# Three more zero matmuls in TensorE's lead-in, and four between the first transform's second group and the first product

## The chip, the cores and the metric

The kernel runs on one core of a Trainium2 chip. The metric is the device time of one execution in microseconds (us), as a median over several executions; lower is better.

## The reference, cut to what matters

```
def A(x, w_r, w_i):                     # x: 2048 x 512
    X = rfft2(x.astype(float32))        # over both axes: 2048 x 257
    return irfft2(X * (w_r + 1j * w_i)).astype(bfloat16)

def B(x, w1, b1, w2, b2):               # w1: 2048 x 1792, w2: 1792 x 2048
    h = layernorm(x)                    # over the 512 columns
    u = gelu(einsum("bsd,sf->bdf", h, w1) + b1)
    return (einsum("bdf,fs->bds", u, w2) + b2).transpose(0, 2, 1)

g = sigmoid((x * gate_w).sum(-1, keepdims=True))
out = g * A(x) + (1 - g) * B(x)
```

Inputs, weights and output are bfloat16; A and B get the same x.

## The kernel before, in words

**The layout.** The 2048 rows are cut into sixteen blocks of 128, j = 4q + r, where r is the row's number modulo 4. Everything that belongs to one r (four blocks, 512 KB of x) is loaded and handled together, in the order r = 0, 1, 2, 3.

**The layer-norm branch.** VectorE (DVE) takes mean and variance of each block (L461, L462), ScalarE (ACT) takes the root (L471), DVE the reciprocal and shift (L475, L476). The normalized block h is then written by ACT (L485), or by DVE (L479) for blocks 0, 8 and 4. The *products* of the first matrix multiplication (L655) are 14 column tiles ft times 16 blocks j = 224 matmuls of 128x512. The first six tiles go pairwise through the blocks as these come: twelve products for blocks 0 and 8, six for block 4, six for 12, six for 1 and so on. Each finished tile goes through gelu on ACT (L669). The second multiplication (L929) is again 224 such matmuls.

**The Fourier branch.** For each r, DVE makes four sums and differences of the blocks (L493, L494, L499, L500), and TensorE (PE) multiplies them by tables in four groups dq of four matmuls (L512 to L515, function `fa`): the *first transform* of r. Each group fills one of two PSUM buffers with the tag "fa", which ACT empties (L518). DVE then works on the results (L525 to L532, radix4 at L551 to L564). The second transform (L620 to L623, evicted at L627), the reversal of the filter's rows (L705), the inverse transforms (L841 to L844, L837 and L911 to L915) follow, with DVE's multiplication and butterflies between them.

**The lead-in.** Before any data are there, `warm` (L350 to L353) issues thirteen 128x512 matmuls on a tile that DVE has set to zero (L314). Nothing reads their result. A second zeroed tile, `s9` (L315, L319), gets its real contents only late in the kernel, by a DMA (L803).

**What sets the order.** All work is written down as tasks with an engine, a book duration, what they read and write, a priority (lower goes first), and the PSUM buffers that they take and give back (`add`, L149). `order` (L170) plays these through in book time before the program is built: whenever an engine is free, the ready task of the lowest priority number starts. What an engine executes on the chip is this order, fixed; only waits on the chip decide when. A task that follows one of another engine is ready 0.15 book-us after it, and on DVE 0.10 after one of its own. Book durations that the text uses: 0.42 for each zero matmul (L355), 0.2158 for a product (`mm(512)`), 0.33 for a group of the first transform, 0.49 for its eviction. Priorities on PE: lead-in -5, first transform 0, second transform 2, inverse transforms 3 and 4, reversal 5, products 10 and up, so products fill the time that all else leaves free.

Of the kernel before, what the change touches and what calls it, by code (L numbers as in the profile page):

```python
# [14 lines left out]
F32 = mybir.dt.float32  # L15

P = 128
S = 2048
D = 512
# [117 lines left out]
class Plan:  # L137
# [11 lines left out]
    def add(self, eng, dur, emit, reads=(), writes=(), prio=0.0, alloc=(), free=(), nbytes=0, after=()):  # L149
        t = Task()  # L150
        t.eng, t.dur, t.emit, t.prio = eng, dur, emit, prio
        t.alloc, t.free, t.nbytes = tuple(alloc), tuple(free), nbytes
        t.users, t.end, t.ready = [], None, 0.0
        deps = set(after)
        for k in reads:
            if k in self.last_w:
                deps.add(self.last_w[k])
            self.readers.setdefault(k, []).append(t)
        for k in writes:
            if k in self.last_w:  # L160
                deps.add(self.last_w[k])
            deps.update(self.readers.get(k, ()))
            self.last_w[k] = t
            self.readers[k] = []
        deps.discard(t)
        t.deps = deps
        self.tasks.append(t)
        return t
# [79 lines left out]
def act(n, ptr=0):  # L248
    return 0.065 + 0.09 * ptr + n / 1200.0
# [12 lines left out]
def kernel(  # L262
# [14 lines left out]
    V, A, T = nc.vector, nc.scalar, nc.tensor  # L277
# [15 lines left out]
    def ps(shape, dt, tag, bufs):  # L293
        return psum.tile(shape, dt, tag=tag, name=tag, bufs=bufs)
# [4 lines left out]
    add = pl.add  # L299
    t = {}  # L300
# [49 lines left out]
    def warm():  # L350
        pw = ps([P, D], F32, "fa", 2)
        for _ in range(NWARM):
            T.matmul(pw[:], lhsT=t["warm"][:, 0:P], rhs=t["warm"], start=True, stop=True)  # L353
    NWARM = 13
    add("PE", 0.42 * NWARM, warm, reads=["warm", "xs"], writes=["warmed"], prio=-5, alloc=["fa"], free=["fa"])  # L355

    def presq():
# [23 lines left out]
    for b in range(2):  # L381
        add(("SP", "ACT")[b], 0.5, ld_w1(0, slice(b, 4, 2), (None, A)[b]), writes=[("w1", 0, 4 * b), ("w1", 0, 4 * b + 8)], prio=(0.5, -4)[b],
            alloc=() if b else ["wa"], nbytes=393216, after=[a0])
# [62 lines left out]
    for r in range(4):  # L446
# [3 lines left out]
        for b, qs in enumerate(groups):  # L450
# [32 lines left out]
            for j in js:  # L483
                if j in HACT:
                    add("ACT", act(512, 2), lambda j=j: A.activation(t["h"][:, j // 4, j % 4, :], t["x"][:, j // 4, j % 4, :], ActF.Identity,  # L485
                                                                  bias=t["nmr"][:, j:j + 1], scale=t["rstd"][:, j:j + 1]),
                        reads=xb + [("rstd", *g)] + mvk, writes=[("h", j)], prio=-0.5 + 0.1 * r)
# [19 lines left out]
        for dq in range(4):  # L507
            def fa(r=r, dq=dq):
# [8 lines left out]
                free=["xf"] if dq == 3 else ())  # L517
            add("ACT", act(512), lambda r=r, dq=dq: A.copy(t["X"][:, :, r, :, dq, :], t["pa", r, dq][:]),  # L518
                reads=[("pa", r, dq)], writes=[("X", r, dq)], prio=0, free=["fa"])
# [77 lines left out]
    for lt in (1, 0):  # L597
# [5 lines left out]
        writes=[("Z", 0, 0), ("Z", 0, 1)], prio=3.1)  # L603
# [8 lines left out]
    for lt in (0, 1):  # L612
        for e in (0, 2, 1, 3):
            for c in range(2):
# [13 lines left out]
                           t["pb", lt, e, c][:].rearrange("p s b i -> p s i b"))  # L628
                add("ACT", act(512), fbev, reads=[("pb", lt, e, c)], writes=[("B", lt, e)], prio=1.8, free=[tag])


    def biasT():
        pb = t["pbias"] = ps([P, 32], F32, "fa", 2)
        T.matmul(pb[:, 0:NFT], lhsT=t["b1b"][:], rhs=t["flip"][:, P - NFT:P], start=True, stop=True)
        for r in range(4):
            T.matmul(pb[:, 16 + 4 * r:20 + 4 * r], lhsT=t["b2b"][:, r::4], rhs=t["flip"][:, P - 4:P], start=True, stop=True)
# [26 lines left out]
    for n, (ft, j) in enumerate(order):  # L663
# [3 lines left out]
                       prio=10 + n * 1e-3, alloc=[bank] if j == jorder[0] else (), free={NF - 1: ["wa"], NF + 3: ["wb"], NFT - 1: ["wb"]}.get(ft, ()) if last else ()))  # L667
        if last:
            gelus.append(add("ACT", act(512, 1), lambda ft=ft: A.activation(  # L669
                t["gl"][:, ft, :], t["u", ft][:], ActF.Gelu_apprx_tanh, bias=t["b1f"][:, ft:ft + 1], scale=1.0),  # L670
                reads=[("u", ft), "b1f"], writes=[("gl", ft)] + ([("xf", (ft - 6) // 4)] if ft >= 6 else []), prio=0.5,
                free=[bank]))
# [3 lines left out]
    for r in range(4):  # L676
# [3 lines left out]
            reads=["gw"], writes=xk, prio=6)  # L680
# [5 lines left out]
        reads=[("xg", q, r) for q in range(4) for r in range(4)], writes=["g"], prio=5, after=gelus[0:1])  # L686
# [25 lines left out]
    def wfn():  # L712
# [6 lines left out]
        reads=["pwn"], writes=wtk, prio=3, free=["fa"])  # L719
# [90 lines left out]
    for lt in range(2):  # L810
# [5 lines left out]
        if lt == 0:  # L816
            add("SP", 0.5, lambda: dma(t["B"][0:1, 0].rearrange("p e (c v) l -> p (e c) (v l)", c=2), t["s8"][:]),
                reads=["s8"], writes=[("T", 0, 0), ("T", 0, 1)], prio=0, nbytes=8192)
# [83 lines left out]
    for grp in groups:  # L902
        for j in grp:
# [19 lines left out]
            for n, cs in enumerate(parts):  # L923
                for ft in range(NFT):
                    def m2(ft=ft, j=j, q=q, r=r, n=n, cs=cs):
# [6 lines left out]
                        alloc=[("acc", "fa")[n]] if ft == 0 else (), after=m1t[-16:-15] if ft == 0 else ())  # L932
# [24 lines left out]
            else:  # L957
# [6 lines left out]
                for n, cs in enumerate(parts):  # L964
                    def fin(j=j, n=n, cs=cs):
# [3 lines left out]
                        free=[("acc", "fa")[n]])  # L969
# [42 lines left out]
```

## Time and profile before

| | |
|---|---|
| time, median of 3 runs | 135.7 us (135.46 to 136.01) |
| span of the profiled execution, first to last instruction | 134.9 us |
| PE busy | 128.1 us, 95% of the span |
| DVE busy | 115.2 us, 85% |
| ACT busy | 82.3 us, 61% |
| mean granted TensorE clock | 0.987 |
| HBM read and written | 20.93 MB and 2.10 MB |

The profile gives the span of the profiled execution and no total time of its own; the median of the timed runs lies 0.8 us above that span. In the profile, a row of the timeline has start, duration, engine, line, operation, output and inputs, shape and count, and in brackets how long the engine had stood idle before and what ended that. Matmuls are pipelined, so durations of neighbours overlap; the pace of PE is the distance between their starts. The table of stretches lists, for each stretch of time, the busy time of each engine, then the granted TensorE clock (PEclk), the share of DMA and its GB/s. The chain of waits follows the work that ended last back to what released it.

### The profile page before, as it was taken

The numbers are of one execution on the slowest core, as the hardware profiler recorded it, in microseconds if no ns is written. First come the engines' busy times: TensorE is split into PE (matmuls) and PEld (weight loads), VectorE is DVE, ScalarE is ACT, GpSimd is POOL, SyncE is SP. The second block draws the span as 40 slices with busy tenths as digits, with TensorE's granted clock in tenths as the row PEclk, the third lists the DMA queues.
The fourth block names the chain that finished last, engine by engine and source line by source line (L and its number), as shares of the span: only waits on it lengthen the run. The fifth ranks groups of instructions, "written<-read, shape, count | busy, mean of one in ns | idle before, by whom it ended". The sixth has DMA issues, their size and how long they took to land.

```text
span 134.9 us, 2171 instructions
## 1 busy us (share of the span) xinstructions
PE 128.1 (95%) x763; PEld 72.2 (53%) x777; DVE 115.2 (85%) x294; ACT 82.3 (61%) x159; POOL 0.2 (0%) x4
## 2 busy tenths in 40 slices
PE   6949999999999999999999999999999999999991
PEld 2234465645544576644445445557766755655590
DVE  2987999999999994499999999998696899999531
ACT  4036679998999999994222007237993776574200
POOL 0000000000000000000000000000000000000000
PEclk9995999999999999999999999999999999999999
DMA  4999999996399928999701940000000003303021
GB/s 128 246 367 363 362 355 346 345 233 84 100 351 322 150 39 317 373 418 404 293 6 35 415 174 0 5 2 2 0 0 0 5 0 155 152 9 158 16 101 39
DMA packets 17110, 23.18 MB, mean 172 GB/s; under 512 B 1078, under 2 KB 14540, under 8 KB 17100
## 3 DMA queue, kind: packets, MB, share of 16 engines
q1 hardware_dynamic: 16540, 22.39, 51.2%
q10 hardware_dynamic: 560, 0.66, 1.5%
q8 instruction: 6, 0.10, 0.3%
q14 instruction: 4, 0.03, 0.1%
HBM read 20.93 MB, written 2.10 MB: 171 GB/s over the span
## 4 chain that ended last, share of the span: by engine, by line
PE 61%; DMA 27%; SPq 9%; issue 1%; DVE 0%
PE acc L929 35%; PE acc L655 14%; DMA wa<-in_B_w_dram 12%; DMA wt<-in_A_w_i_dram 9%; SPq L303 9%; DMA wt<-in_A_w_r_dram 5%; PE fa L837 1%; PE fb L837 1%; PE fa L929 1%; PE fa L623 1%; PE fb L623 1%; PE fb L911 1%; PE fa L911 1%; PE fa L705 0%; PE fa L841 0%
## 5 line engine op out<-in xcount | busy, mean ns | idle before, releaser
L929 PE MATMUL acc<-gl,wb 128*128 128x512 bf16 (+1 forms) x123 | 31.0, 373 | 0.3
L655 PE MATMUL acc<-h,wb 128*128 128x512 bf16 x124 | 29.0, 379 | 0.1
L929 PE MATMUL acc<-gl,wa 128*128 128x512 bf16 (+1 forms) x94 | 23.4, 372 | 0.1
L929 PEld LDWEIGHTS <-wb 128*128 128x128 bf16 x136 | 14.8, 114 | 9.9 <-DMA wb<-in_B_w_dram 0.3
L655 PEld LDWEIGHTS <-wb 128*128 128x128 bf16 x128 | 12.4, 98 | 13.1
L655 PE MATMUL acc<-h,wa 128*128 128x512 bf16 x62 | 17.7, 394 | 1.0 <-DMA wa<-in_B_w_dram 0.9
L949 ACT ACTIVATE x<-acc,ombb,omg 128x512 bf16<-128x512 f32 x14 | 10.7, 776 | 11.2 <-PE acc L929 11.2
L929 PEld LDWEIGHTS <-wa 128*128 128x128 bf16 x102 | 11.5, 114 | 8.8
L655 PEld LDWEIGHTS <-wa 128*128 128x128 bf16 x96 | 9.8, 102 | 11.2 <-issue 1.3
L669 ACT ACTIVATE gl<-acc,b1f 128x512 bf16<-128x512 f32 x12 | 8.6, 715 | 8.9 <-PE acc L655 8.8
L461 DVE BATCH_NORM_STATS2 stats<-x 128x6 f32<-128x512 bf16 x16 | 10.8, 672 | 3.0 <-DMA x<-in_A_x_dram 3.0
L518 ACT CAST X<-fa 128x512 bf16<-128x512 f32 x16 | 8.9, 585 | 5.5 <-PE fa L515 5.3
L485 ACT ACTIVATE h<-x,nmr,rstd 128x512 bf16<-128x512 bf16 x13 | 9.6, 804 | 1.2 <-DVE nmr L476 1.2
L683 ACT ACTIVATE x<-x 128x512 bf16<-128x512 bf16 x16 | 10.2, 673 | 0.0
L655 PE MATMUL fb<-h,wa 128*128 128x512 bf16 x31 | 9.4, 395 | 0.0
L920 ACT ACTIVATE eo<-fa,g 128x512 bf16<-128x512 f32 x8 | 5.5, 686 | 4.8 <-DVE x L955 3.8
L353 PE MATMUL fa<-xp 128*128 128x512 bf16 x13 | 5.5, 612 | 1.2 <-DVE xp L314 1.2
L955 DVE TENSOR_TENSOR x<-x,eo 128x512 bf16<-128x512 bf16 x14 | 5.4, 418 | 0.5 <-ACT x L949 0.5
L920 ACT ACTIVATE eo<-fb,g 128x512 bf16<-128x512 f32 x8 | 5.5, 683 | 0.0
L808 ACT CAST s<-fa 8x512 bf16<-8x512 f32 x1 | 0.6, 574 | 7.9 <-PE fa L806 7.9
L627 ACT CAST B<-fb 128x512 bf16<-128x512 f32 x8 | 5.3, 661 | 0.0
L627 ACT CAST B<-fa 128x512 bf16<-128x512 f32 x8 | 5.2, 650 | 0.0
(167 smaller groups left out, 236.3 us busy)
## 6 DMA issues: line engine op xcount, KB each, us to landing
wb<-in_B_w_dram SPq DMA_DIRECT2D x8, 512.0 KB
wb<-in_B_w_dram SPq DMA_DIRECT2D x4, 1024.0 KB
wa<-in_B_w_dram SPq DMA_DIRECT2D x3, 1024.0 KB
wa<-in_B_w_dram SPq DMA_DIRECT2D x3, 768.0 KB
x<-in_A_x_dram SPq DMA_DIRECT2D x3, 512.0 KB
out_dram<-x SPq DMA_DIRECT2D x3, 512.0 KB
rot<-dft_ti SPq DMA_DIRECT2D x1, 736.5 KB
rot<-dft_ta SPq DMA_DIRECT2D x4, 160.0 KB
```

Source lines behind the costliest of these rows:

```text
L303: (eng or nc.sync).dma_start(out=out_ap, in_=in_ap)
L353: T.matmul(pw[:], lhsT=t["warm"][:, 0:P], rhs=t["warm"], start=True, stop=True)
L461: V.bn_stats(out=t["stats"][:, j, :], in_=t["x"][:, j // 4, j % 4, :])
L485: add("ACT", act(512, 2), lambda j=j: A.activation(t["h"][:, j // 4, j % 4, :], t["x"][:, j // 4, j % 4, :], ActF.Identity, bias=t["nmr"][ ...
L518: add("ACT", act(512), lambda r=r, dq=dq: A.copy(t["X"][:, :, r, :, dq, :], t["pa", r, dq][:]), reads=[("pa", r, dq)], writes=[("X", r, dq ...
L627: A.copy(t["B"][:, lt, e, 2 * c:2 * c + 2, :].rearrange("p s (i b) -> p s i b", b=4), t["pb", lt, e, c][:].rearrange("p s b i -> p s i b"))
L655: T.matmul(t["u", ft][:], lhsT=w[:, j // 4, j % 4, c * P:(c + 1) * P], rhs=t["h"][:, j // 4, j % 4, :], start=(j == jorder[0]), stop=(j == ...
L669: gelus.append(add("ACT", act(512, 1), lambda ft=ft: A.activation(t["gl"][:, ft, :], t["u", ft][:], ActF.Gelu_apprx_tanh, bias=t["b1f"][:, ...
L683: A.activation(t["x"][:, q, r, :], t["x"][:, q, r, :], ActF.Copy, accum_out=t["glog"][:, 4 * q + r:4 * q + r + 1])
L920: A.activation(t["eo", j][:], t["i3", j][:], ActF.Copy, scale=t["g"][:, j:j + 1])
L929: T.matmul(t["y", j, n][:, cs], lhsT=w[:, o, 512 * q + r:512 * q + 512:4], rhs=t["gl"][:, ft, cs], start=(ft == 0), stop=(ft == NFT - 1))
L949: A.activation(tbuf(j).rearrange("p h d -> p (h d)"), t["y", j, 0][:], ActF.Identity, bias=t["ombb2"][:, j:j + 1], scale=t["omg"][:, j:j + 1])
```

## The change

The lead-in gets sixteen zero matmuls in place of thirteen, and its book cost, 0.42 times that number, grows with it. A new PE task `fill` of four matmuls on the zeroed `s9` becomes ready when group dq = 1 of the first transform of r = 0 is done. Its book cost is 0.1, its priority 4, and it takes a PSUM buffer of the tag "fb" and gives it back. No result of it is read.

```
-    NWARM = 13
+    NWARM = 16
     add("PE", 0.42 * NWARM, warm, reads=["warm", "xs"], writes=["warmed"], prio=-5, alloc=["fa"], free=["fa"])
...
+    def fill():
+        pw = ps([P, D], F32, "fb", 2)
+        for _ in range(4):
+            T.matmul(pw[:], lhsT=t["s9"][:, 0:P], rhs=t["s9"][:], start=True, stop=True)
+    add("PE", 0.1, fill, reads=["warm", ("pa", 0, 1)], writes=["warmed"], prio=4, alloc=["fb"], free=["fb"])
```

## Prediction, made before the result was known

> **What bounds the kernel now.** I read the page first (busy shares and slices), then the list of waits, then the timelines of PE and DVE side by side at the places where PE takes DVE's results, and last the chain of waits.
>
> ```profile
> PE   6949999999999999999999999999999999999991
> ...
> DVE  2987999999999994499999999998696899999531
> ...
> PEclk9995999999999999999999999999999999999999
> ```
>
> PE is full from the fourth slice on, and DVE is as full until about 50 us: two engines in lockstep. The granted clock has one dip. In finer stretches (last columns: PEclk, DMA share, GB/s):
>
> ```profile
> 6.00:9.50 3.50, 1.60 (x12) 0.71 (x11) 3.40 (x11) 1.07 (x2) 0.00 (x0) 1.00 1.01 336
> ...
> 10.00:13.00 3.00, 3.00 (x12) 1.43 (x11) 1.98 (x7) 1.71 (x5) 0.00 (x0) 0.50 1.08 363
> ...
> 13.50:16.00 2.50, 2.50 (x13) 1.18 (x12) 2.43 (x6) 1.92 (x4) 0.00 (x0) 1.00 1.08 364
> ```
>
> Half clock from about 9.78 to 13.19 us (the half-microsecond rows at the edges show 0.78 and 0.81), after 3.5 us in which PE was busy for 1.60. The dip follows two waits of PE for DMA, the only waits it has in the list after the lead-in starts:
>
> ```profile
> 7.75 0.22 PE L512 MATMUL fa<-rot,gl 128*128 128x128 bf16 x1 [1.03 <-DMA rot<-dft_ta]
> ...
> 9.43 0.39 PE L655 MATMUL acc<-h,wa 128*128 128x512 bf16 x1 [0.86 <-DMA wa<-in_B_w_dram]
> ```
>
> So the dip costs PE half of 3.41 us, 1.71 us of work. Whether that is 1.71 us of the span depends on how long before PE the data were ready at the next joins. The first transform needs DVE's L500, first for the matmul of L513. Here are DVE's rows, then PE's:
>
> ```profile
> 10.92 0.69 DVE L461 BATCH_NORM_STATS2 stats<-x 128x6 f32<-128x512 bf16 x1 [1.36 <-DMA x<-in_A_x_dram]
> ...
> 16.79 0.42 DVE L500 TENSOR_TENSOR gl<-st 128x512 bf16<-128x512 bf16 x1
> ...
> 22.39 0.42 DVE L500 TENSOR_TENSOR gl<-st 128x512 bf16<-128x512 bf16 x1
> ...
> 31.56 0.41 DVE L500 TENSOR_TENSOR gl<-st 128x512 bf16<-128x512 bf16 x1
> ```
>
> ```profile
> 18.31 0.22 PE L513 MATMUL fa<-rot,gl 128*128 128x128 bf16 x1
> ...
> 23.48 0.22 PE L513 MATMUL fa<-rot,gl 128*128 128x128 bf16 x1
> ...
> 32.21 0.22 PE L513 MATMUL fa<-rot,gl 128*128 128x128 bf16 x1
> ```
>
> DVE ends at 17.21, 22.81 and 31.97; a waiting PE started 0.05 after DVE (L499 ends at 6.70, its reader loads at 6.75). The slack shrinks from 1.05 to 0.62 to 0.19 us. DVE has no idle row from 10.92, where x of r = 1 lands, to 51.96, so nothing that PE gains moves these ends. Further on the chain of waits gives PE's start of the reversal to a DMA:
>
> ```profile
> 37.31 11.13 DMA wt<-in_A_w_i_dram
> ...
> 48.46 1.20 DMA wt<-in_A_w_i_dram
> 49.66 0.00 issue
> 49.66 0.38 PE fa L705 x2
> ```
>
> There the slack is zero. **The kernel is bound by PE's work, but until about 50 us a faster PE only waits longer for DVE and DMA.**
>
> **The change, part by part.**
>
> *Three more matmuls in the lead-in.* The thirteen start 0.43 us apart (1.21 to 6.30), the pace of the dip, although the clock column says 1.00 there; I take the spacing. Three more cost 0.65 us at 0.215 (full pace; eight products of L929 take from 117.97 to 119.69) or 1.28 at half. The lead-in's end of 6.72 becomes 7.4 to 8.0. PE waits until 7.75 for the table anyway, so the price on the first groups is 0 to 0.25 us. Their evictions and the root behind them on ACT have over a microsecond before DVE takes that root, since DVE stands until 10.92. I take 0.
>
> *Four in the gap.* The first two groups' last matmul starts at 8.30, so PE is free at 8.41; the first product starts at 9.43 when its weights land. Four at 0.215 fill 0.86 of these 1.02 us; at half pace they take 1.71 and push the product back by 0.7. The trace has no such row in this place, so these are my bounds: 0 and 0.7. I take 0, since PE ran at full pace at 7.75 to 8.41; and 0.7 would go into the waits below. Behind `fill` in PE's queue stand that product and the groups dq = 2 and 3; its buffer is next used by PE itself, near 12.1.
>
> *The dip.* In the stretch before it, 6.00 to 9.50, PE would be busy for 1.60 + 0.65 + 0.86 = 3.11 us of 3.50. I expect no dip then: PE gains 0 to 1.71, and I take 1.71. The Trainium skill (TensorE: Matmul & The Clock Gate, "What's actually happening") has the clock halved after an idle window of about 3.4 us, in windows that run free. The dip's length agrees; but this trace halves the clock after a partly busy stretch, with no idle row over 1.03. By the page read strictly the fillers could save nothing, by the trace up to 1.71. The sum below is the same by either.
>
> *The order.* This part has to be followed in the book, which fixes order and is no time. The lead-in ended in book time at 0.16 + 13 x 0.42 = 5.62, and the groups began at 5.91, when DVE's sums were there. With sixteen it ends at 6.88: the groups end at 7.54 and not 6.57, `fill` at 7.64. Before, PE waited until 6.80 for h of block 0; now it doesn't. Twelve products and two groups (3.25) end at 10.89 and not 10.05; before, PE then waited for block 4 until 10.26. So the book's PE runs 0.63 late, **three products**, and finds no idle time afterwards to make that good. DVE's book isn't moved beyond 11.81: ACT's root for blocks 4 and 12 slips ahead of two evictions, and DVE's h of block 4 ahead of one block's statistics, but the sum of DVE's work up to there is the same. The first transform of r = 1 is due at 14.09 in both. Before it came after all six products of block 1 (14.15), now after three (14.14). As transforms go ahead of products, each later transform, reversal and inverse has three products fewer ahead of it, and these come at the end. From 117.97 on PE does nothing but products: three there are 3 x 0.215 = 0.65 us.
>
> *The sum.* Without the dip and without the three products, PE would reach the transform of r = 1 at 18.26 - 1.71 - 0.65 = 15.9; data are there at 17.21 (start 17.25). The next one 5.16 later is at 22.41, where L513 must wait until 22.86; 8.73 more is 31.6, where it waits until 32.02. Before it was 32.21: 0.19 us is left of 1.71. At 49.66 that goes into the wait for the filter. If the dip stayed, PE would still come to r = 3 about when its data do. So: -1.71 from the dip, +1.71 given back in waits, **+0.65** for products moved to the end, -0.05 for small gaps. Span 134.9 becomes 135.5; with the 0.8 us between span and median, **136.3 us** against 135.7.
>
> **The rivals.**
>
> *PE keeps what it gains.* If PE's own work is the bound all through (95% busy speaks for it, and the lack of listed waits), 1.71 is saved and the order costs nothing: 134.0. Against it: the 0.19 us at r = 3 and the DMA at 49.66. It needs DVE's chain to start before 10.92, which the change doesn't touch. Chance 0.16, a partial saving included.
>
> *The order doesn't slip*, or PE makes the three products good in some wait before 118 us: 135.6. For it: the book is close, three products of 0.216 against 0.63. Against it: waits of PE are fixed to places in the order. Chance 0.14.
>
> *Slower still, by ACT.* ACT is without idle from 32.14 to beyond 58. The second gelu (L669, at 32.14) needs a product that now falls behind the first groups of r = 3. ACT would wait there, with the gelu's 0.58 us still to do. If no other ACT work moves back in exchange, its evictions of the second transform, and then DVE, which waits for them at 57.18, are 0.58 late, and so are the last inverse transforms at 103.88: 136.3 + 0.58 = 136.9. It decides if the number of gate passes (L683) ahead of the first eviction at 46.90 stays the same; the book should let one fall back. Chance 0.20.
>
> **How the numbers follow.** Forecast 0.50, with a range of its own from 135.9 to 136.7; the rivals 0.16, 0.14 and 0.20. A measurement of this kernel can tell about 0.5%, 0.68 us, from no change. Faster than 135.0 is the first rival, 0.16. Above 136.4 lie the third rival and four tenths of the forecast, 0.40. The rest, 0.44, is within 0.5%. For the range I leave out the first rival and the upper end of the third: 135.3 to 137.0. It takes in the 0.7 of a half-pace fill only in part, since the waits absorb it.
>
> **What would show it.** PEclk without 0.50 near 10 to 13 us (the dip). PE rows with new waits for DVE at L512 or L513, near 17.2, 22.8 and 32.0, and the latter no more than 0.2 us earlier. Three products of block 1, not six, ahead of the transform of r = 1. The reversal again near 49.66. From the start of the last inverse group (L911 at 117.69) to the last matmul, three products more. Wrong it would be if L513 of r = 3 came a microsecond earlier, or if DVE's chain no longer began at 10.92.

## The result, and the profile after

The changed kernel takes **137.56 us** (median of 11 executions, 136.35 to 138.11); the kernel before, run beside it, 135.86 us (11 executions). The ratio is 1.0124, interval 1.0087 to 1.0161. On a second chip (`after_again` below) it was 1.0079 (1.0035 to 1.0122). It is slower, and slower than the forecast of 136.3 us. The ratios of this document leave out executions that took over 1.5% longer than the fastest of the same kernel.

The profiled span grew by 0.8 us, 134.9 to 135.7. First the page's rows for PE, DVE and the granted clock, as they were shown of the kernel before, and the shares of the chain that ended last:

```profile
span 135.7 us, 2183 instructions
...
PE   6979889999999999999999999999999999999991
...
DVE  3976999999999998199999999996786899999431
...
PEclk9999999999999999999999999999999999999999
...
PE 70%; DVE 15%; DMA 9%; SPq 2%; issue 1%; ACT 1%
```

The dip of the clock is gone, and DVE, which had 0% of this chain before, has 15%. The stretches where the dip was (PE, PEld, DVE, ACT, POOL busy; PEclk; DMA share; GB/s):

```profile
6.00:9.50 3.50, 2.73 (x17) 1.38 (x16) 3.29 (x11) 0.74 (x2) 0.00 (x0) 1.00 1.02 341
10.00:13.00 3.00, 3.00 (x20) 1.69 (x19) 1.62 (x6) 1.66 (x4) 0.00 (x0) 1.00 1.08 370
13.50:16.00 2.50, 2.46 (x12) 1.16 (x12) 2.40 (x9) 1.61 (x3) 0.00 (x0) 1.00 1.08 362
```

PE does 20 matmuls in the second stretch, where it did 12. The added matmuls themselves lie beside waits for DMA. Behind the longer lead-in PE still waits 0.77 us for the table of the first transform. The timeline of PE shows the four (L635) between the second group and the first product:

```profile
8.24 0.22 PE L512 MATMUL fa<-rot,gl 128*128 128x128 bf16 x1 [0.77 <-DMA rot<-dft_ta]
...
8.89 1.03 PE L635 MATMUL fb<-s 128*128 128x512 bf16 x4
...
9.85 0.39 PE L661 MATMUL acc<-h,wa 128*128 128x512 bf16 x1
```

Then the joins of the first transform. DVE's rows, and PE's rows of the same stretches (lines behind the change are six higher than before, L655 is now L661):

```profile
11.31 0.69 DVE L461 BATCH_NORM_STATS2 stats<-x 128x6 f32<-128x512 bf16 x1 [1.92 <-DMA x<-in_A_x_dram]
...
17.17 0.42 DVE L500 TENSOR_TENSOR gl<-st 128x512 bf16<-128x512 bf16 x1
...
22.77 0.42 DVE L500 TENSOR_TENSOR gl<-st 128x512 bf16<-128x512 bf16 x1
...
31.86 0.42 DVE L500 TENSOR_TENSOR gl<-st 128x512 bf16<-128x512 bf16 x1
```

```profile
17.31 0.23 PE L512 MATMUL fa<-rot,gl 128*128 128x128 bf16 x1 [0.80 <-DVE gl L499]
...
17.65 0.23 PE L513 MATMUL fa<-rot,gl 128*128 128x128 bf16 x1
...
23.25 0.23 PE L513 MATMUL fa<-rot,gl 128*128 128x128 bf16 x1
...
32.33 0.23 PE L513 MATMUL fa<-rot,gl 128*128 128x128 bf16 x1
```

PE now stands for DVE at 17.31, and each L513 starts 0.05 to 0.06 us after DVE's L500 has ended: the slack of 1.05, 0.62 and 0.19 us is used up. The reversal starts at 49.59 (49.66 before). One wait is new and was not forecast. In the chain of waits:

```profile
72.84 0.70 ACT gl L675
73.53 0.52 SPq L303
74.05 0.06 issue
74.11 4.09 DMA s<-X
78.19 0.14 issue
78.33 0.38 PE fa L812
```

This is the line matmul (L806 before), which multiplies the contents of `s9`. Before, it came at 80.25 without a wait of PE in the list; now it stands at 78.33, and PE's timeline has `[0.35 <-DMA s<-X]` behind it. Its two small loads now go out ahead of the last load of w2 on SP, and so it stands 14 products earlier in PE's order.

In the order, 27, 44 and 78 products stand ahead of the first transform of r = 1, 2 and 3, where 30, 47 and 81 stood; 134 ahead of the reversal of the second half, where it was 138; 341 and not 343 ahead of the first of the last inverse groups, and 379, not 384, ahead of the last one.

**What the span doesn't hold.** The metric is longer than the span, and by how much turned out to depend on the kernel. In every execution of the changed kernel the time less the span is 2.2 us (2.17 to 2.27); in 115 executions of the kernel before it is 1.8 (1.73 to 1.86). So 0.45 us of the result is in no row of the timeline.

### The profile page after: what moved, and what is told of

The parts are those of the page before. It is cut to its first block, busy times and chain, and to the rows that moved or that the text cites. A ratio compares the mean times of both kernels' runs of the same rounds, so it can differ in the third digit from the quotient of the medians.

```text
span 135.7 us, 2183 instructions
## 1 busy us (share of the span) xinstructions
PE 128.7 (95%) x770; PEld 72.2 (53%) x784; DVE 115.3 (85%) x294; ACT 82.3 (61%) x159; POOL 0.2 (0%) x4
## 4 chain that ended last, share of the span: by engine, by line
PE 70%; DVE 15%; DMA 9%; SPq 2%; issue 1%; ACT 1%
PE acc L935 30%; PE acc L661 22%; DMA x<-in_A_x_dram 6%; DVE stats L461 5%; DMA s<-X 3%; DVE mv L462 2%; SPq L303 2%; DVE gl L494 1%; PE fa L843 1%; DVE st L493 1%; PE fa L623 1%; PE fb L843 1%; PE fb L623 1%; PE fb L661 1%; PE fa L935 1%
## 5 line engine op out<-in xcount | busy, mean ns | idle before, releaser
L661 PE MATMUL acc<-h,wb 128*128 128x512 bf16 x124 | 28.8, 379 | 0.1
L661 PEld LDWEIGHTS <-wb 128*128 128x128 bf16 x128 | 12.4, 98 | 13.3
L661 PE MATMUL acc<-h,wa 128*128 128x512 bf16 x61 | 16.8, 379 | 0.2
L935 PEld LDWEIGHTS <-wa 128*128 128x128 bf16 x102 | 11.4, 114 | 8.4
L661 PEld LDWEIGHTS <-wa 128*128 128x128 bf16 x96 | 9.4, 98 | 9.4 <-DMA wa<-in_B_w_dram 0.4
L661 PE MATMUL fb<-h,wa 128*128 128x512 bf16 x32 | 9.5, 379 | 0.0
L353 PE MATMUL fa<-xp 128*128 128x512 bf16 x16 | 6.3, 575 | 1.2 <-DVE xp L314 1.2
L512 PE MATMUL fa<-rot,gl 128*128 128x128 bf16 x16 | 3.5, 220 | 1.6 <-DVE gl L499 0.8
```

The lines of the kernel that those rows point to most:

```text
L661: T.matmul(t["u", ft][:], lhsT=w[:, j // 4, j % 4, c * P:(c + 1) * P], rhs=t["h"][:, j // 4, j % 4, :], start=(j == jorder[0]), stop=(j == ...
L935: T.matmul(t["y", j, n][:, cs], lhsT=w[:, o, 512 * q + r:512 * q + 512:4], rhs=t["gl"][:, ft, cs], start=(ft == 0), stop=(ft == NFT - 1))
```

## The experiments

**The theory** after the comparison: the seven matmuls cost nothing; the order that their book cost brings does, by three products at the end and by the early line matmul. **The rivals**: the matmuls themselves cost the time, by delaying the start or by the clock; or the changed start of VectorE and ScalarE does. Kernels of one batch ran on one chip, and each ratio is against the kernel before on that chip. "Join" is the first L513 of r = 3, "landing" the DVE row at which x of r = 1 has come.

### The seven matmuls without their book cost, and the book cost without the matmuls

```
instr_only   add("PE", 0.42 * 13, warm, ...)     add("PE", 0.0, fill, ...)      # 16 and 4 issued
order_only   NWARM = 13; add("PE", 0.42 * 16, warm, ...); fill without matmuls
```

> The sixteen and the four zero matmuls are issued, but the book charges the lead-in 0.42 x 13 and the four nothing, so the order of all else is that of the kernel before (30, 47 and 81 products ahead of the transforms of r = 1, 2, 3). Theory (the order costs, the matmuls don't): no dip, 0 to 0.2 us faster than before, since the gain of 1.71 goes into waits for DVE. Rival (the zero matmuls themselves cost, by a later first product or by what they displace): as slow as the changed kernel, +1.7 us.

> Thirteen zero matmuls and no fill are issued, but the book charges 0.42 x 16 and 0.1 for an empty task, so the order is that of the changed kernel (27, 44 and 78 products ahead of the transforms). Theory: 0.65 us for three products at the end plus whatever else the order does, so +0.65 to +1.7 us against before, with the dip in the clock still there. Rival (the zero matmuls cost): within 0.2 us of before.

Measured: the matmuls with the old order 0.9999 (0.9966 to 1.0032), span 134.9; the new order without the matmuls 1.0049 (1.0014 to 1.0085). **The matmuls cost nothing that 0.3% can tell; the order does.** The spans say the same: their medians are 134.8 and 135.2 us, and 134.6 for the kernel before. Another 0.46 us of the new order's time lies outside the span (2.25 against 1.79 us), and the last experiments are about that part. The new order's profile also shows PE waiting for the filter, which the other had not (without the fill, lines are four higher than before):

```profile
49.19 0.39 PE L709 MATMUL fa<-wt,flip 128*128 128x256 bf16 x2 [0.79 <-DMA wt<-in_A_w_i_dram]
...
51.24 0.38 PE L709 MATMUL fa<-wt,flip 128*128 128x256 bf16 x2 [0.80 <-DMA wt<-in_A_w_i_dram]
```

Such a wait stands in four of the eighteen profiles, two with the order of before from the transforms on (lines_early and third_charged, below) and two with the changed one, and in neither profile of the changed kernel. The four are also the longest of the eighteen profiled spans, 136.0 to 136.9 us. So the wait isn't tied to either order.

### The line matmul put back, and put early alone

```
lines_late    lined = add("SP", 1.0, lines, ..., prio=50, ...)         # the changed kernel otherwise
lines_early   instr_only, and the last ldw2 on SP also reads "s9"
```

> The changed kernel, but the two small loads into s9 get priority 50 in the book in place of 0, so that they go behind the last load of the second weights, as before the change, and the matmul that reads them stands after 262 products and not after 248. Theory A (the early line matmul, which waits 0.35 us for its data in the profile of the changed kernel, is part of the excess over 0.65): 0.3 to 1.0 us faster than the changed kernel. Theory B (three products alone): the same as the changed kernel.

> All seven matmuls issued, the book and with it every product in the order of the kernel before; only the small loads of the lines go out ahead of the last w2 load on SP, as they do in the changed kernel, so that the line matmul (L812) stands 14 products earlier. Theory that the early line matmul is a term of its own: TensorE waits 0.35 to 0.6 us for the DMA of s ahead of L812, the profile's span is 0.3 to 0.5 us over the 134.9 of the kernel with the order of before and the seven matmuls, and the ratio is about 1.003. Rival, that this wait only takes the place of the wait of 0.23 to 0.31 us for wb that the order of before has near 77.1 us: ratio 0.999 to 1.001. If the half microsecond outside the span comes with the products' order and not with the lines, the time less the span stays at 1.8 us.

Measured: put back, 1.0047 (1.0013 to 1.0082), where `order_only` with the early line matmul had 1.0049 on the same chip; put early alone, 1.0010 (0.9978 to 1.0042). The wait itself is there whenever the line matmul is early, as here in the second kernel:

```profile
78.92 0.38 PE L812 MATMUL fa<-s,tb 128*8 128x512 bf16 x1 [0.59 <-DMA s<-X]
```

With the line matmul late, PE's gap there, beyond the pace of its starts, is 0.10 us; early it is 0.49 to 0.75 in five profiles, 0.39 to 0.65 more. The gap for wb near 77 us that the order of before has and the early one lacks is only 0.02 to 0.12 us. My expectation put it at 0.23 to 0.31, since some rows of PE there show three matmuls where four weights were loaded: a matmul is missing from the trace. So the early line matmul costs up to 0.6 us at its own place, but the medians don't show it, nor did my 1.003 come; how much of it reaches the end is looked at with the last two profiles.

### More products ahead of the transforms

If products left for the end cost 0.216 us each, products taken earlier must gain. The book's cost of the first 72 products was lowered, so that more of them fit ahead of the transforms:

```
ahead_195   add("PE", 0.195 if n < 72 else mm(512), lambda ft=ft, j=j: m1(ft, j), ...)   # 32, 51, 87
ahead_19    0.19                                                                          # 33, 52, 88
ahead_17    0.17                                                                          # 35, 54, 92
ahead_dip   as ahead_195, NWARM = 13 and no fill
```

All but the last issue the seven matmuls, at the book cost of the thirteen.

> The zero matmuls of the changed kernel, charged as in instr_only, and the book's cost of the first 72 products is 0.195 in place of 0.2158, so that 32, 51 and 87 products go ahead of the transforms of r = 1, 2, 3, and 350 and not 343 ahead of the last inverse transforms. Theory (waits for DVE eat the gain of the clock, and products moved ahead of them use it): six to seven products of 0.215 fewer at the end, 1.0 to 1.5 us faster than before. Rival (PE's own work is the bound, waits are no matter): as instr_only, within 0.2 us of it.

> As ahead_195 with a book cost of 0.190: 33, 52 and 88 products ahead of the transforms, 355 ahead of the last inverse transforms. Theory: up to five products fewer at the end than ahead_195 where PE has room for them, 0 to 0.8 us faster than ahead_195; if PE now comes to the joins last, no more gain or some loss.

> All seven matmuls, the first 72 products booked at 0.17 us, so that 35, 54 and 92 products of block 1 stand ahead of the three later transforms' matmuls (before 30, 47 and 81) and 14 products fewer follow the inverse transform's start. If every product taken ahead of the filter's DMA is worth 0.216 us, span 134.9 - 14 x 0.216 = 131.9 and a time near 133.7. If the wait for that DMA is used up with the ten products of the run at 0.19 (which reached it at 50.48 us), further products only push the transforms back: 134.8 to 135.4, as that run (135.0), and the filter's reversal starts past 51.3 us.

> The order of ahead_195 (32, 51 and 87 products ahead of the transforms), but thirteen zero matmuls and no fill, so the clock may dip as before. Theory (the clock's gain is real, and only an order with more products ahead can use it): where the clock dips, PE reaches the transforms after their data and the 1.7 us show, so 0.4 to 1.5 us slower than ahead_195. Rival (the order alone brings the gain, the clock is no matter): within 0.2 us of ahead_195.

Measured: 0.9937 (0.9900 to 0.9973), **0.9877 (0.9847 to 0.9908)**, 0.9939 (0.9910 to 0.9968) and 0.9937 (0.9903 to 0.9971): the direction is confirmed four times, and 135.0 us at 0.19 beats both kernels. The first gained 0.86 us, where I had expected 1.0 to 1.5. At 0.17 the time was 135.72 us, above the 134.8 to 135.4 that I had put for a wait that is used up, and far from the 133.7 of the plain count; 0.36 us of it lie outside the span beyond what the others have there, as the last experiments show. Within the span the two are equal: from the landing to the start of PE's last eight matmuls it takes 118.79 us at 0.17 and 118.80 at 0.19, and 119.84 in instr_only. So seven products more ahead of r = 3, or eleven, gained the same 1.05 us, less than 0.216 each. The page's chain of the kernel at 0.17 and the list of PE's waits, without that for the first zeroed tile, say why:

```profile
PE 80%; DMA 14%; SPq 2%; issue 1%; DVE 0%
```

```profile
PE acc L661 <- DMA wa<-in_B_w_dram: 0.5, 1, 0.5
PE acc L661 <- DVE h L479: 0.3, 1, 0.3
PE fa L512 <- DVE rstd L475: 0.2, 1, 0.2
```

DVE is out of the chain, where it still has 24% at 0.19, and PE hardly waits: what is taken ahead from here on only pushes the joins back. The join at 0.17 stands 22.52 us behind the landing, where it stood 21.03 in instr_only.

The last of the four tells what the matmuls are worth. Three of its 12 executions dip (mean clock 0.986 or 0.987) and take 136.26, 136.65 and 136.77 us; the other nine take 134.76 to 136.27, with a median of 135.55. **In this order executions that dip take 1.1 us longer.** In the kernel before they take 0.3 to 0.5 us longer (medians of 136.68 against 136.39 on one chip, 136.77 against 136.29 on another, 0.5 apart on the other two). Three executions are few, and such executions may also have had their data later; no profile of `ahead_dip` with a dip exists. Over all executions its ratio equals that of ahead_195.

### Each half of the added matmuls, and the book's first step

```
lead_only       NWARM = 16 at the book cost of 13, no fill
fill_only       NWARM = 13, fill at book cost 0
third_charged   all seven; the book charged for 15, fill at 0
```

> Sixteen zero matmuls in the lead-in, no fill, order of the kernel before. One look, for the clock: if the fill is what keeps the clock up, there is a stretch at half clock of about 3.4 us after the first products' wait; if the longer lead-in suffices, none. The time is that of before in both cases, within 0.3 us by the theory.

> The four fill matmuls alone, thirteen in the lead-in, order of before. If the lead-in's three are what keeps the clock up, dips of the granted clock stay in a quarter to a third of the executions (3 or 4 of 12 with a mean clock near 0.987). If the fill's four are, none of 12 dips. The median is that of the kernel before within 0.3% either way (136.2 to 136.7 where before is 136.4), since a dip costs only 0.3 to 0.5 us in this order.

> All seven matmuls, the book charged for fifteen lead-in matmuls and no fill: the order of the products at every later join is that of before (30, 47, 81, filter at 138 to 142, inverse at 343), and only a few of the first transform's evictions on ScalarE and statistics on VectorE change places, as they do in the changed kernel. Theory that the time comes from the products behind the filter: ratio 0.997 to 1.003. Rival, that it comes from the changed start of VectorE and ScalarE: 1.005 or more. The time less the span tells whether the half microsecond outside the span (1.8 in the order of before, 2.2 to 2.3 in the changed one) comes with that start (2.2) or with the rest (1.8).

Measured: the first ran once, 137.41 us, without a dip; that is 0.85 us over the median of before, where I had expected 0.3 at most, but a single execution says little. The four alone 0.9996 (0.9967 to 1.0025), and none of 12 executions dips. That is the second of the two cases that I had put down, that the four suffice; at the rate of the kernel before on that chip, 6 of 35, no dip in 12 would come by chance about one time in ten. The kernel before dips in 30 of 115, and the kernels with all seven in none of 132. (Two of the 132, at a mean clock of 0.76 and 0.95, and one of the 115, at 0.606, lost clock in another way; no profile of these exists.)

Charged for 15, the order gave 1.0008 (0.9977 to 1.0039). It differs from that of before by single products at the joins, but at the start by one square root (L471) on ScalarE alone, which is taken one place earlier; VectorE's start is the old one. So this run hardly tests the rival of the changed start. What does is the distance from the landing to the join, which the changed start leaves as it was.

Two profiles show best what holds the first third. Their landings lie 1.94 us apart (DVE's row, then PE's; the four alone, then charged for 15):

```profile
9.52 0.69 DVE L461 BATCH_NORM_STATS2 stats<-x 128x6 f32<-128x512 bf16 x1 [0.20 <-DMA x<-in_A_x_dram]
...
30.54 0.23 PE L513 MATMUL fa<-rot,gl 128*128 128x128 bf16 x1
```

```profile
11.46 0.69 DVE L461 BATCH_NORM_STATS2 stats<-x 128x6 f32<-128x512 bf16 x1 [1.92 <-DMA x<-in_A_x_dram]
...
32.48 0.23 PE L513 MATMUL fa<-rot,gl 128*128 128x128 bf16 x1
```

30.54 - 9.52 = 21.02, and 32.48 - 11.46 = 21.02. The distance is 21.02 or 21.03 in every profile with 78 or 81 products ahead and no dip, ten besides these two, five of them with the changed order and its start. With the dip (the kernel before) it is 21.29. The join is DVE's, the rival of the changed start falls as far as this join, and the dip costs 0.27 us there.

### The changed kernel again, and VectorE's program length

```
after_again    the changed kernel
after_313      the changed kernel; V.memset(b2b) in two halves            # VectorE 313
instr_314      instr_only with the same cut                               # VectorE 314
instr_312      instr_only; eps set by nc.gpsimd.memset, not V.memset      # VectorE 312
ahead_17_313   ahead_17 with the same cut                                 # VectorE 313
```

What the time has beyond the span sorts the first thirteen kernels in two groups, 1.8 and 2.2 us. The traces have one more difference along the same line: VectorE's rows, its separate semaphore waits counted, are 313 in the first group and 312 in the second. The theory: the shorter program is slow outside the span. The rival: the changed order is.

> The changed kernel once more, beside the kernel before on the same chip as the next two. Theory (only the order costs): the ratio of order_only and lines_late, 1.003 to 1.008, so some 0.4 to 1.1 us over before. Rival (something of 1 us beside the order, which order_only did not have): 1.2% or more over before, as in the first comparison of the changed kernel.

> The changed kernel, with one zeroing of VectorE at its start (the 128x512 tile b2b) cut into two halves, so that VectorE's program has 313 instructions as in the kernel before, not 312. Theory that the 0.45 us outside the span comes with VectorE's 312: time less span 1.8 us in every execution, not 2.2, the span as in the changed kernel (135.4), and a ratio 0.003 under that of the changed kernel on the same chip as before (1.008), so about 1.005. Rival, that it comes with the changed order itself: time less span stays at 2.2 us and the ratio at 1.008.

> The seven matmuls with the order of before, and the same zeroing of VectorE cut in two: 314 instructions. If only the program with 312 is slow outside the span, time less span stays at 1.8 us and the ratio within 0.997 to 1.003. If any other length than 313 is slow, 2.2 us and a ratio of 1.003.

> The seven matmuls with the order of before, and one zeroing (eps) given to GpSimd, so that VectorE's program has 312 instructions. Theory of VectorE's 312: time less span 2.2 us although the order is that of before, ratio about 1.003. Rival, that the changed order itself is the cause: 1.8 us and a ratio within 0.997 to 1.003.

> The kernel with the first 72 products booked at 0.17 us, which had 312 instructions on VectorE and 2.16 us outside its span, with the same zeroing cut in two: 313. Theory of VectorE's 312: time less span 1.8 us, the median 0.35 to 0.4 us under the 135.72 of that kernel, about 135.35, ratio 0.991. Rival: 2.16 us and a ratio of 0.994 as before.

Measured (time less span, median and extremes over all executions):

| kernel | order | VectorE rows | time less span, us | ratio |
|---|---|---|---|---|
| after_again | changed | 312 | 2.23 (2.19 to 2.29) | 1.0079 |
| after_313 | changed | 313 | 1.85 (1.81 to 1.94) | 1.0027 (0.9995 to 1.0059) |
| instr_312 | before | 312 | 2.15 (2.12 to 2.19) | 1.0008 (0.9982 to 1.0033) |
| instr_314 | before | 314 | 1.83 (1.82 to 1.89) | 1.0009 (0.9978 to 1.0040) |
| ahead_17 | 92 ahead | 312 | 2.16 (2.12 to 2.21) | 0.9939 |
| ahead_17_313 | 92 ahead | 313 | 1.80 (1.74 to 1.85) | 0.9895 (0.9854 to 0.9936) |

**The rival falls.** One instruction more takes 0.38 and 0.36 us away in two orders, and one less adds 0.35 in the order of before. With 136.84 us the changed kernel is then 0.5 us over the kernel before on that chip (136.31), though the interval of the ratio takes in 1; the 1.0079 of `after_again` lies at the upper end of the 1.003 to 1.008 that I had put for the order alone. The ratio of 1.003 that I expected of instr_312 did not show: the median of its spans was 134.2 against 134.5, about as much shorter as the 0.35 that it lost outside. Behind the landing, though, nothing is shorter with 312: to the start of PE's last eight matmuls it takes 119.79 us in instr_312 and 119.85 in instr_314, 120.44 in the changed kernel and 120.45 in after_313. So the shorter spans of instr_312 would come from ahead of the landing, which varies by 2 us anyway. That the step is time lost, and not time moved out of the span, is likely and not shown. The kernel at 0.17 with 313 took 134.99 us, less than the 135.35 that I had put.

Two of these profiles also have the same landing, so that the order can be read alone: after_313, where the cut memset moves lines up by two more, then instr_312.

```profile
10.46 0.69 DVE L463 BATCH_NORM_STATS2 stats<-x 128x6 f32<-128x512 bf16 x1 [1.11 <-DMA x<-in_A_x_dram]
...
130.91 1.04 PE L937 MATMUL fa<-gl,wb 128*128 128x256 bf16 x8
```

```profile
10.46 0.69 DVE L461 BATCH_NORM_STATS2 stats<-x 128x6 f32<-128x512 bf16 x1 [0.94 <-DMA x<-in_A_x_dram]
...
130.25 1.04 PE L935 MATMUL fa<-gl,wb 128*128 128x256 bf16 x8
```

PE's last eight matmuls start **0.66 us** later with the changed order. Three products are 3 x 0.2158 = 0.65. In both profiles the first transform of r = 3 starts at 31.16, with 78 and 81 products ahead of it, and all 784 matmuls are recorded. From there to the last eight, PE's gaps beyond its pace add up to 1.98 and 1.97 us: the line matmul's gap is 0.4 us longer with the changed order, and others, above all those ahead of the inverse transforms near 92 to 98 us, are as much shorter. So the three products alone are left. It isn't the luck of one pair: from the landing it takes 120.44, 120.45 and 120.61 us in the three profiles of the changed order that have no wait for the filter, and 119.79, 119.84 and 119.85 in the three with all seven matmuls, the order of before and no such wait. The medians of the spans are 0.4 to 0.6 us longer than before in each of the four kernels with the changed order.

## Why the prediction was wrong, point by point

**The dip goes** (right, and worth less than its name). No execution of a kernel with the four matmuls dipped. But the profile shown was one of the quarter in which the kernel before dips at all, so in the median there was little to gain, some 0.1 us (a quarter of 0.3 to 0.5). The Trainium skill (TensorE: Matmul & The Clock Gate, "What's actually happening") ties the halved clock to an idle window of about 3.4 us; the trace of before had no idle row over 1.03 us once the lead-in had begun and still dipped, and no execution with four matmuls in a gap of 1.02 us did, so the filling of short gaps counts, by these runs.

**The added matmuls cost nothing** (right, to 0.3%): 0.9999 (0.9966 to 1.0032) with the order of before.

**What PE gains is given back in waits for DVE** (right, to a tenth): L513 of r = 3 at 32.33, bound by DVE, 21.02 us behind the landing where the forecast had 21.10; the same distance in twelve profiles shows it for more than one execution. One of the prediction's signs of being wrong did come: DVE's chain began at 11.31 and not at 10.92. But the landing varies between profiles, from 9.52 to 11.46 us with the order of before and from 10.03 to 11.31 with the changed one, so nothing points to the change. The second half of the step, that the filter's DMA takes the rest at 49.66, was too strong: PE reached that place at 49.59 without a wait. In the profile before the chain ran through that DMA, in this one it doesn't.

**The order slips by three products, +0.65** (right in size): 78 for 81 at the join; 0.66 between two profiles of one landing. Where I said three more after the last inverse group there were five, because products change places with the inverse groups as well; the end counts what is left after the join.

**Overlooked in the order**: the line matmul, 14 products earlier and waiting for its loads. Its own gap is 0.39 to 0.65 us longer, but between the two profiles of one landing nothing of it is left (0.66 less 0.65), since other gaps of PE are shorter.

**The sum of the span** (right): 135.5 forecast, 135.7, 135.4 and, in the profile with the cut memset, 134.9 measured. The medians of the spans were 135.4 against 134.8 on the second chip: +0.6, as forecast. On the first the hit is in part luck: there the kernel before, with 1.8 us outside, had a span of some 134.1 (an estimate from its median of 135.86), so that 134.9 was a high start; and half of the 0.8 us by which the profiled span grew is the landing, 0.39 later.

**From span to median** (this step failed): "with the 0.8 us between span and median". The step took the median of three executions less the span of another for a constant. The kernel before has 1.8 us outside its span in every execution, so the profiled one took about 136.7 us, one of its slower ones, with a dip and a landing at 10.92. The changed kernel has 2.2. With that, 135.5 becomes 137.7, and 137.56 was measured. Of the 1.4 us in between, 1.0 is the base that the profiled execution gave, and 0.45 is what the changed kernel has more outside. One instruction of VectorE's program takes 0.38 of that away again; no row of the profile before could show it.

**The rivals.** PE keeping its gain (134.0) and no slip (135.6) fell with 32.33 and with the count of products. The one by ACT fell too: the butterflies that it was to delay start at 57.63, 57.75 before.

**The account.** 0.65 for products, nothing seen of the line matmul, 0.45 outside the span, about -0.1 for dips: some 1.0 us. The second chip measured 1.1 (0.0079 x 136.56), the first 1.7. The rest of the first, 0.7 us, stays open; the lower end of its interval, 1.0087, is 1.2 us. The kernel before had a median of 135.86 us there, and 136.31 to 136.56 on the four other chips; the changed kernel had 137.56 and 137.67.

## What to carry to other kernels

An instruction that hides in a wait is free on the chip and not in a planner: give fillers no book cost, and compare the planned order before and after. A gain on one engine is worth what is left after the next join, so measure the distance from a landing to the join in several executions: where it is constant (21.02 us here), the other engine holds it, and moving work ahead of that join pays until the wait is used up. Compare times with times and spans with spans; what lies between them belongs to the kernel.

## What the runs showed of the hardware that was not expected

- The time outside the span changes in a step with the length of VectorE's program: 2.12 to 2.30 us with 312 rows in five kernels, 1.73 to 1.94 with 313 or 314 in twelve. The cause isn't settled. In each trace a last code fetch of 8 KB starts 0.3 to 1.3 us after the span's end. The Trainium skill (Runtime: NRT & Kernel Launch, "Instruction fetch mechanics") has engines fetch their code in blocks, at a cost that is mostly hidden. That the step is such a block's end was not tried, and the traces don't speak for it: all eighteen hold the same number and sizes of code fetches, and the last one is equally late with 312 and with 313 rows (0.96 and 0.97 us in the changed kernel, 0.31 and 0.30 at 0.17).
- The granted clock dips in about one execution in four of the same program (30 of 115, at a mean of 0.984 to 0.987). In the one profile with a dip it halves for 3.41 us. Such executions take 0.3 to 0.5 us longer where VectorE holds the next joins, and 1.1 (three executions) where more products stand ahead of them.
- The landing of x for r = 1 varies from 9.52 to 11.46 us between profiles, and the join follows it one to one.
